# Splitting the first wq load by partitions: 16 rows of partitions ahead of the other 112

## The chip, the cores and the metric

One Trainium2 chip, one core of it. The metric is device time in microseconds for one execution of the whole kernel, as the median of several runs. Beside it there is one profiled execution, from which every duration below comes.

## What is computed

One token (x, 1 x 1024) goes through a layernorm, and the result feeds two branches whose outputs are added to x: attention over the last 4096 positions of a KV cache, and an MLP.

```python
xn = layernorm(x)
# branch A: 32 query heads, 4 KV heads, head size 128, window W = 4096
q = xn @ wq                                  # wq: 1024 x 4096
scores = q . k_cache[:, :, Sk - W:] * 128**-0.5
o = softmax(scores) . v_cache[:, :, Sk - W:]
a = o @ wo                                   # wo: 4096 x 1024
# branch B
y = layernorm(xn)
b = gelu(y @ w1 + b1) @ w2 + b2              # w1: 1024 x 3584, w2: 3584 x 1024
out = x + a + b
```

All inputs are bf16. With one token every weight is used once, so some 40 MB have to be brought in: wq, wo and the two cache windows take 8 MB (wo, wq) and 4 MB (K, V) each, w1 and w2 7 MB each.

## The kernel before

All large loads are issued by SP on one queue, in an order written out by hand; each has a semaphore that rises by 16 when it has landed. `load_rows` (L164 to 170, its DMA is L166) takes a weight matrix seen as 128 partitions x rows: for wq, partition p holds rows 8p to 8p+7 of the matrix, so "row" below means one of the 8 rows of 4096 numbers (8 KB) that a partition holds. `load_cache` (L172, L173) loads K or V.

The order on SP:

1. wq, in two chunks: one row for all partitions (1 MB), then seven rows (7 MB), into `WA` (L175).
2. After POOL has made its constants (`C["selq"]`, L210): K into `KT` (L211), w1 into `W1` (L212), V into `V` (L213).
3. After the q product (`C["q"]`, L323): w2 into `WA`, over wq (L324).
4. After the product with w1 (`C["h"]`, L424): wo in five loads, into `W1` and `KT` (L425 to 427).
5. The result (L583).

ACT issues three small loads on its own queue: x (four rows of 512 B, into partitions 0, 32, 64 and 96 of `XB4`, L191), b1 (four rows of 1,792 B into the same partitions of `B1R`, L192) and later b2 (L246).

The compute follows the loads. DVE transposes x (L242), POOL, PE, ACT and DVE make the layernorm's statistics, and `XNTb` (L261) holds the normalised x. `wide_product` (L306 to 318, its matmuls are recorded at L283) multiplies it with wq: for each chunk it waits on that chunk's semaphore and runs 8 matmuls for each row. Then q is brought into the block form `QB` (L327 to 350), DVE transposes K in four parts (L355), PE makes the scores (L363 to 371), DVE and ACT the softmax (L375 to 406), PE the product with w1 (L411 to 420), the product with V (L470 to 476), the product with w2 (L516) and at the end the product with wo chunk by chunk (L547 to 575), each waiting for its load. PE products through `go` are recorded at L292.

The lines that tie the wq chunks to the product:

```python
WQ_CHUNKS = [1, 7]
load_rows(WA, wq_p, WQ_CHUNKS, NQ, s_wq)
wide_product(WA, [(0, 1), (1, 8)], NQ, s_wq, XNTb, 512, [4, 5], "q")
```

Of the kernel before, what the change touches and what calls it, by code (L numbers as in the profile page):

```python
# [19 lines left out]
KC = D // 128  # L20
NQ = 4096
# [2 lines left out]
PB = 128  # L24
NEG = -1.0e20
PV_UNROLL = 5
WQ_CHUNKS = [1, 7]
W1_CHUNKS = [8]
W2_CHUNKS = [28]
WO_CHUNKS = [16, 8, 4, 3]  # L30
# [22 lines left out]
def bass_parallel_sum__sliding_block_cached__mixer_channel_mlp__decode_kernel(  # L53
# [18 lines left out]
    pe, dve, act, pool, sp = nc.tensor, nc.vector, nc.scalar, nc.gpsimd, nc.sync  # L72

    def sems(name, n):
        return [nc.alloc_semaphore(f"{name}{i}") for i in range(n)]

    s_x, s_b1, s_b2, s_res, s_out = (nc.alloc_semaphore(n) for n in ("s_x", "s_b1", "s_b2", "s_res", "s_out"))
    s_wq = sems("s_wq", len(WQ_CHUNKS))
    s_w1 = sems("s_w1", len(W1_CHUNKS))
# [10 lines left out]
    def sb(name, shape, d):  # L90
        return nc.alloc_sbuf_tensor(name, shape, d)

    f32, bf16 = dt.float32, dt.bfloat16
    WA = sb("WA", [128, KC * NQ], bf16)
# [21 lines left out]
    XNTb = sb("XNTb", [128, 8], bf16)  # L116
# [38 lines left out]
    wq_p = A_wq.rearrange("(p r) n -> p r n", r=KC)  # L155
# [8 lines left out]
    def load_rows(dst, src, chunks, width, semaphores, first=0, c0=0, off=0):  # L164
        for j, n in enumerate(chunks):
            sp.dma_start(  # L166
                dst[:, off + c0 * width: off + (c0 + n) * width].rearrange("p (c n) -> p c n", c=n),
                src[:, first + c0: first + c0 + n, :],
            ).then_inc(semaphores[j], 16)
            c0 += n  # L170
# [1 line left out]
    def load_cache(dst, src, sem):  # L172
        sp.dma_start(dst[:, :], src[0, :, SK - W:SK, :].rearrange("g (m b) d -> m g (b d)", m=32)).then_inc(sem, 16)  # L173

    load_rows(WA, wq_p, WQ_CHUNKS, NQ, s_wq)  # L175
    def d(ins):
        return DVE.mark(ins)

# [103 lines left out]
    def held(out, rhs, w, pos, size, start, stop, load=False):  # L282
        return pe.add_instruction(mybir.InstMatmult(  # L283
            name=nc.get_next_instruction_name(), engine=PEE, ldweights=load,
            start_tensor_calc=start, stop_tensor_calc=stop, tile_size=size, tile_position=pos,
            ins=[pe.lower_ap(rhs), pe.lower_ap(w, for_matmul_weights=True)], outs=[pe.lower_ap(out)]))
# [18 lines left out]

    def wide_product(weights, chunks, width, semaphores, vec, n, banks, name):  # L306
        for j, (k0, k1) in enumerate(chunks):
            pe.wait_ge(semaphores[j], 16)
            for k in range(k0, k1):
                w = vec[:, k:k + 1].to_broadcast([128, 32])  # L310
                for a in range(4):
                    pe.ldweights(w, tile_position=(0, 32 * a))  # L312
                for b in range(2):
                    for a in range(4):
                        lo = k * width + (2 * a + b) * n
                        last = held(PS[32 * a:32 * a + 32, banks[b] * 512: banks[b] * 512 + n], weights[:, lo:lo + n], w,
                                    (0, 32 * a), (128, 32), k == 0, k == KC - 1)
        C[name] = PE.mark(last)

    hinted = pe.mark_branch_hint_location()  # L320
    wide_product(WA, [(0, 1), (1, 8)], NQ, s_wq, XNTb, 512, [4, 5], "q")

    sp.wait_ge(PE.sem, C["q"])  # L323
    load_rows(WA, w2_p, W2_CHUNKS, D, s_w2)  # L324
# [290 lines left out]
```

## Time and profile before

| what | value |
|---|---|
| median of three runs | 98.87 us (98.68 to 98.9) |
| profiled execution, its own time | 98.68 us |
| its span in the profile | 97.4 us |
| moved by DMA | 39.88 MB, mean 410 GB/s over the span |
| busy: PE, PEld, DVE, ACT, POOL | 53.7, 14.0, 41.3, 11.5, 8.2 us |
| wq, first chunk: issue to landing | 1,024 KB, 4.5 us |
| wq, second chunk | 7,168 KB, 21.2 us |
| K, w1, V, w2: issue to landing | 25.7, 41.9, 51.1, 48.2 us |

The time is that of the device from start to end of one execution; the span is what the profile's records cover, and 1.28 us lie around it. Busy times overlap each other. The landing time of a load runs from its issue on SP, so it holds the wait behind earlier loads on the same DMA engines too. Stretches of the trace give, for any interval, the busy time of each engine, the clock granted to PE, the mean share of the 16 DMA engines that was taken, and GB/s; a DMA packet is booked in the stretch in which it starts.

### The profile page before, as it was taken

To read this page: it belongs to the slowest core of one execution; us is meant where nothing else is said; L and a number is where in the kernel's file an instruction comes from. 1 tells how busy PE (TensorE), PEld (TensorE's weight loads), DVE (VectorE), ACT (ScalarE), POOL (GpSimd) and SP (SyncE) were. 2 spreads that over 40 slices of the span, in tenths; PEclk is the share of its full clock that TensorE was granted. 3 is DMA by queue.
4 is the path that set the end of the run, shared out by engine and by line. 5 is a ranking of instruction groups with operands and counts; after the bars stand their busy time and mean duration, and the time that the engine had idled before them with its cause. 6 is when DMAs were issued, how large, how long until landed. Compare 5 with 4: busy or idle time off the path is not lost.

```text
span 97.4 us, 886 instructions
## 1 busy us (share of the span) xinstructions
PE 53.7 (55%) x361; PEld 14.0 (14%) x218; DVE 41.3 (42%) x43; ACT 11.5 (12%) x22; POOL 8.2 (8%) x33
## 2 busy tenths in 40 slices
PE   0000241007933929663366189875999577877862
PEld 0000220001200002001010022112333111212320
DVE  0001221000065899999996630599941500020021
ACT  0000517000022000000000449400000000000021
POOL 6776211000000000000000000000000000000000
PEclk9999999999996555799985555999999999999999
DMA  2998888999999988889999999888899999799980
GB/s 77 707 401 377 380 377 378 401 542 431 417 431 562 448 377 377 377 377 565 404 431 431 431 569 401 377 377 377 377 542 427 431 431 431 323 431 397 422 365 11
DMA packets 1614, 39.88 MB, mean 410 GB/s; under 512 B 190, under 2 KB 204, under 8 KB 460
## 3 DMA queue, kind: packets, MB, share of 16 engines
q1 hardware_dynamic: 1588, 39.85, 95.6%
q8 instruction: 1, 0.02, 0.1%
q10 hardware_dynamic: 24, 0.01, 0.0%
q14 instruction: 1, 0.01, 0.0%
HBM read 39.86 MB, written 0.00 MB: 409 GB/s over the span
## 4 chain that ended last, share of the span: by engine, by line
DMA 55%; DVE 22%; PE 12%; POOL 5%; issue 3%; SPq 2%; ACT 1%; POOLq 0%
DMA KT<-in_A_wo_dram 29%; DMA KT<-in_A_k_cache_dram 26%; DVE KT L355 18%; PE PS L292 8%; PE PS L283 3%; DVE MX L377 2%; SPq L166 2%; POOL F L206 1%; POOL B1R L188 1%; DVE MR L388 1%; ACT Q L381 1%; POOL QB L198 1%; DVE ORow L581 0%; PE PS L385 0%; POOL I L199 0%
## 5 line engine op out<-in xcount | busy, mean ns | idle before, releaser
L355 DVE STREAM_TRANSPOSE KT<-KT 128x4096 bf16<-128x4096 bf16 x4 | 17.4, 4413 | 1.1 <-DMA KT<-in_A_k_cache_dram 1.1
L283 PE MATMUL PS<-KT,QB 128*128 128x512 bf16 x32 | 10.4, 483 | 7.6 <-DVE KT L355 7.6
L283 PE MATMUL PS<-WA,XNTb 128*32 128x512 bf16 x64 | 6.1, 553 | 7.4 <-DMA WA<-in_A_wq_dram 7.4
L292 PE MATMUL PS<-V,WA 128*128 (+1 forms) x31 | 7.9, 381 | 1.6 <-DVE LR L430 1.4
L292 PE MATMUL PS<-WA,GT 128*32 x56 | 6.7, 382 | 2.5 <-issue 1.8
L292 PE MATMUL PS<-W,YTb 128*32 x64 | 6.7, 432 | 0.8 <-issue 0.7
L253 PE MATMUL PS<-XT,onesf 128*128 128x16 f32 x2 | 0.6, 384 | 10.6 <-POOL XT L251 10.6
L327 DVE CAST Q<-PS 128x512 bf16<-128x512 f32 x1 | 0.7, 692 | 11.9 <-PE PS L283 11.9
L242 DVE STREAM_TRANSPOSE XT<-XB 128x256 bf16<-128x256 bf16 x1 | 0.6, 626 | 9.4 <-DMA XB<-in_A_x_dram 9.4
L367 PEld LDWEIGHTS <-QB 128*128 128x128 bf16 x16 | 1.8, 114 | 18.3 <-DVE KT L355 13.8
L406 DVE STREAM_TRANSPOSE WA<-WA 128x4096 bf16<-128x4096 bf16 x1 | 4.4, 4433 | 0.0
L283 PE MATMUL PS<-MRow,ML 128*128 128x512 bf16 x8 | 3.6, 626 | 0.7 <-DVE QB L348 0.7
L557 DVE COPY KT<-PS 128x512 f32<-128x512 f32 x1 | 0.7, 692 | 7.7 <-PE PS L292 7.7
L292 PEld LDWEIGHTS PS<-V,WA 128*128 (+1 forms) x32 | 3.1, 96 | 5.9 <-issue 2.9
L292 PE MATMUL PS<-W,OT 128*32 128x512 bf16 x48 | 2.9, 380 | 1.6 <-DMA W<-in_A_wo_dram 0.9
L520 DVE TENSOR_TENSOR OD<-PS,D 128x128 f32<-128x128 f32 x1 | 0.3, 292 | 8.2 <-PE PS L518 8.2
L381 ACT ACTIVATE Q<-PS 128x512 f32<-128x512 f32 x1 | 0.6, 597 | 24.0 <-DVE MX L377 24.0
L298 PE MATMUL PS<-identf 128*128 128x512 f32 (+4 forms) x10 | 3.4, 454 | 0.0
L558 ACT ACTIVATE KT<-PS 128x512 f32<-128x512 f32 x1 | 0.6, 597 | 22.4 <-PE PS L292 22.4
L402 ACT ACTIVATE WA<-PS,NMB 128x1024 bf16<-128x1024 f32 (+1 forms) x2 | 3.1, 1535 | 1.3 <-DVE NMB L397 1.3
L312 PEld LDWEIGHTS <-XNTb 128*32 128x32 bf16 x32 | 1.1, 130 | 11.8 <-DMA WA<-in_A_wq_dram 8.3
L377 DVE TENSOR_REDUCE MX<-PS 128x1 f32<-128x2048 f32 x1 | 2.3, 2291 | 0.8 <-PE PS L283 0.8
(104 smaller groups left out, 46.3 us busy)
## 6 DMA issues: line engine op xcount, KB each, us to landing
WA<-in_A_wq_dram SPq DMA_DIRECT2D x1, 7168.0 KB, 21.2
W<-in_B_w_dram SPq DMA_DIRECT2D x1, 7168.0 KB, 41.9
WA<-in_B_w_dram SPq DMA_DIRECT2D x1, 7168.0 KB, 48.2
KT<-in_A_k_cache_dram SPq DMA_DIRECT2D x1, 4096.0 KB, 25.7
V<-in_A_v_cache_dram SPq DMA_DIRECT2D x1, 4096.0 KB, 51.1
W<-in_A_wo_dram SPq DMA_DIRECT2D x1, 4096.0 KB, 20.0
W<-in_A_wo_dram SPq DMA_DIRECT2D x1, 2048.0 KB, 24.5
WA<-in_A_wq_dram SPq DMA_DIRECT2D x1, 1024.0 KB, 4.5
```

Source lines behind the costliest of these rows:

```text
L166: sp.dma_start(dst[:, off + c0 * width: off + (c0 + n) * width].rearrange("p (c n) -> p c n", c=n), src[:, first + c0: first + c0 + n, :], ...
L188: C["b1z"] = p(pool.memset(B1R[:, :], 0.0))
L283: return pe.add_instruction(mybir.InstMatmult(name=nc.get_next_instruction_name(), engine=PEE, ldweights=load, start_tensor_calc=start, st ...
L292: return pe.add_instruction(mybir.InstMatmult(name=nc.get_next_instruction_name(), engine=PEE, ldweights=load, start_tensor_calc=start, st ...
L298: pe.matmul(bank(3, 0, n), lhsT=identf[:, :], rhs=identf[:, 0:64].unsqueeze(1).to_broadcast([128, n // 64, 64]), start=True, stop=True)
L312: pe.ldweights(w, tile_position=(0, 32 * a))
L355: C["kt"].append(d(dve.transpose(KT[:, j * W:(j + 1) * W], KT[:, j * W:(j + 1) * W])))
L367: pe.ldweights(w, tile_position=(0, 0))
L377: C["mx1"] = d(dve.tensor_reduce(out=MX[:, 1:2], in_=PS[:, 2048:4096], axis=AX.X, op=ALU.max))
L381: C["s7"] = ACT.mark(act.activation(out=S7, in_=bank(7), func=ACTF.Copy))
L402: C[f"exp{j}"] = C["exp"] = ACT.mark(act.activation(out=PT[:, lo:lo + n], in_=src, func=ACTF.Exp, bias=NMB[:, 0:1], scale=SCALE, accum_out ...
L406: C["PT"] = d(dve.transpose(PT, PT))
```

## The change

The first two wq loads become three. The first takes two rows for partitions 0 to 15 only (256 KB), the second the same two rows for partitions 16 to 127 (1.75 MB), the third the other six rows for all partitions (6 MB). The first two raise the same semaphore, and PE waits for 32 on it before the first two rows' matmuls. The chunks of the product follow: two rows, then six. Nothing else is touched.

```diff
-WQ_CHUNKS = [1, 7]
+WQ_CHUNKS = [2, 6]
+LEAD = 16
...
-    load_rows(WA, wq_p, WQ_CHUNKS, NQ, s_wq)
+    n = WQ_CHUNKS[0]
+    for lo, hi in ((0, LEAD), (LEAD, 128)):
+        sp.dma_start(WA[lo:hi, 0:n * NQ].rearrange("p (c n) -> p c n", c=n), wq_p[lo:hi, 0:n, :]).then_inc(s_wq[0], 16)
+    load_rows(WA, wq_p, WQ_CHUNKS[1:], NQ, s_wq[1:], c0=n)
...
     def wide_product(weights, chunks, width, semaphores, vec, n, banks, name):
         for j, (k0, k1) in enumerate(chunks):
-            pe.wait_ge(semaphores[j], 16)
+            pe.wait_ge(semaphores[j], 32 if j == 0 else 16)
...
-    wide_product(WA, [(0, 1), (1, 8)], NQ, s_wq, XNTb, 512, [4, 5], "q")
+    wide_product(WA, [(0, WQ_CHUNKS[0]), (WQ_CHUNKS[0], KC)], NQ, s_wq, XNTb, 512, [4, 5], "q")
```

## The prediction

> **What bounds the kernel now.** I read the slices of the span first, then the queues, the chain that ended last, the waits, and at last short stretches of the first microseconds, because the change is made there.
>
> ```profile
> DMA  2998888999999988889999999888899999799980
> ...
> q1 hardware_dynamic: 1588, 39.85, 95.6%
> ...
> DMA 55%; DVE 22%; PE 12%; POOL 5%; issue 3%; SPq 2%; ACT 1%; POOLq 0%
> ```
>
> SP's queue (q1) keeps the 16 DMA engines busy for 95.6% of the span. The chain names DVE and PE for a third of the span, but that is only the path by which the releases are followed. The stretches show the same stream without a gap:
>
> ```profile
> 6.00:30.00 24.00, 7.29 (x68) 2.06 (x36) 4.33 (x11) 4.16 (x7) 3.77 (x16) 0.99 0.98 421
> 30.00:60.00 30.00, 17.96 (x66) 3.06 (x34) 23.59 (x12) 4.25 (x7) 0.00 (x0) 0.67 1.01 434
> 60.00:94.00 34.00, 27.16 (x208) 8.40 (x124) 12.71 (x20) 2.60 (x8) 0.00 (x0) 0.99 1.00 426
> ```
>
> Each line gives the stretch, its length, the busy time of PE, PEld, DVE, ACT and POOL, PE's granted clock, and as the last two columns the DMA share and GB/s: from 6 to 94 us the engines are full at 421 to 434 GB/s, some 26.6 GB/s each. A 16 KB packet so takes 16,384 B / 26.6 = 0.62 us. The compute may not break this stream: the wo loads are issued at 65.5 us, after SP's longest wait,
>
> ```profile
> SPq L166 <- PE PS L422: 37.6, 1, 37.6
> ```
>
> and w2 lands only at 27.6 + 48.2 = 75.8, so the queue holds 10 us of work then. The end is therefore: first byte, plus 39.85 MB at the engines' rate, plus the tail from the landing at 95.37 to 97.4. Whatever moves the stream moves the end one for one; nothing else has a price unless it uses up its cover.
>
> The start, in stretches of the same view:
>
> ```profile
> 1.15:1.76 0.61, 0.00 (x0) 0.00 (x0) 0.00 (x0) 0.00 (x0) 0.61 (x1) 1.00 0.00 0
> 1.76:1.90 0.14, 0.00 (x0) 0.00 (x0) 0.00 (x0) 0.00 (x0) 0.14 (x1) 1.00 1.99 468
> 1.90:2.02 0.12, 0.00 (x0) 0.00 (x0) 0.00 (x0) 0.00 (x0) 0.06 (x2) 1.00 0.00 0
> 2.02:2.11 0.09, 0.00 (x0) 0.00 (x0) 0.00 (x0) 0.00 (x0) 0.09 (x1) 1.00 2.11 546
> ```
>
> A packet (one partition's piece of one load) is booked whole where it starts, so shares over 1 are possible. The first issue runs from 0.74 to 1.15 us; no packet starts for another 0.61 us. Then 468 GB/s x 0.14 us = 65.5 KB: eight 8 KB packets start from 1.76 to 1.90, none for 0.12 us, and 546 x 0.09 = 49 KB, six more (two records are missing), start from 2.02. So eight engines start some 0.26 us after the other eight. I read this as descriptors made one row after the other, the first half of the rows for eight engines, the second half for the others: 0.26 us for 64 rows, 4.1 ns a row. [...]
>
> **The change, part by part.** *The start.* The lead load has 16 rows. If each engine gets one, the last is made after 16 x 4.1 = 0.07 us, and the late eight engines start up to 0.26 us earlier: -0.13 us as a mean, -0.26 for the late ones. The stream does not level the engines (in the trace the 56 KB packets of one round start over 0.35 us at 4.5 us, and over 0.54 at 73), so I take -0.26, with -0.13 and -0.34 (the whole spread of starts) as ends.
>
> *The lead load's writes.* Here lies the main term. [...] The lead load puts 16 engines on partitions 0 to 15, four groups. If a group's path takes one engine's rate, four share it: 4 x 0.62 = 2.48 us for the packet instead of 0.62, and all 16 engines lose 1.86 us, which a stream at full rate cannot win back. Does a path limit exist? One event bears on it. B1R's four 1,792 B rows go to partitions 0, 32, 64 and 96. [...]
>
> ```profile
> 10.89:10.93 0.04, 0.04 (x2) 0.04 (x2) 0.00 (x0) 0.04 (x1) 0.00 (x0) 1.00 9.94 4301
> 11.07:11.08 0.01, 0.01 (x1) 0.01 (x1) 0.00 (x0) 0.01 (x1) 0.00 (x0) 1.00 13.75 5734
> 11.11:11.20 0.09, 0.09 (x1) 0.01 (x1) 0.00 (x0) 0.09 (x1) 0.00 (x0) 1.00 7.36 3186
> ```
>
> The three packets in the first stretch took 9.94 x 16 x 0.04 / 3 = 2.12 us each; the one that started at 11.07 took 13.75 x 16 x 0.01 = 2.20. One stream packet, just one, was 0.08 us longer beside some 0.14 us of foreign writing. Priced by this row (0.6 of the foreign time) the lead loses 3 x 0.62 x 0.6 = 1.1 us; with no path limit, nothing; with sixteen rows on one path, 15 x 0.62 = 9.3, for which nothing speaks. I take 1.86, since four engines stand on each path for their whole packet, and keep 0 (the first rival) and 1.1 as ends.
>
> [...]
>
> *The load of partitions 16 to 127.* 112 rows of 16 KB are seven packets for an engine, 4.3 us. If the rows stay with the engines that have them now, no path is shared and the price is 0. [...] Ends 0 and 2.2; no row tells which split holds, so I take 0.6, the middle of the first two outcomes.
>
> *One more load.* SP issues three instead of two: one issue is 0.41 us (the two wq issues took 0.87 together), and it ends at 1.97 instead of 1.56. Behind it on SP is only the k_cache load, which waits for POOL until 6.44. In the rings it adds one completion packet (9 ns): 0.02 us. ACT's issue of x starts at 1.98, just behind; even 0.5 us there is covered, next paragraph.
>
> *The wait for 32 on s_wq[0], and the chunks of 2 and 6.* PE now needs 2 MB instead of 1 MB first: about 1.76 + 5.0 to 8.0 = 7 to 10 us. PE's first q matmul is at 14.04, set by x's layernorm, so 4 us of cover remain. Nothing but q itself stands behind that wait on PE. Two rows (2.1 us) then run before the six land, near 22 to 24 us. Six rows instead of seven behind that landing: 5.10 x 6/7 = 4.4 us, so q ends 0.7 us earlier against it. That is worth nothing: w2's issue, which waits for q, joins a queue full until 58 us, and DVE already stands idle for the K cache:
>
> ```profile
> PE PS L283 <- DMA WA<-in_A_wq_dram: 7.4, 1, 7.4
> ...
> DVE KT L355 <- DMA KT<-in_A_k_cache_dram: 1.1, 1, 1.1
> ```
>
> If x came 6 us later than now, this cover would be gone and q would be late by the rest.
>
> **Sum.** -0.26 + 1.86 + 0.6 + 0.02 = +2.2 us. The profiled execution took 98.68 (span 97.4 and 1.28 around it), so 100.9; the median of the three runs is 98.87, so 101.1, which I give. With the ends of this case: 98.87 + 1.1 - 0.34 = 99.6 to 98.87 + 1.86 + 2.2 - 0.13 = 102.8.
>
> **Rivals.** *Faster: no shared path.* Every engine writes to any partition at its own rate; then only the start is left: -0.26 + 0.02, 98.6 (98.5 to 98.8 with the ends). For it: packets of 8 KB and of 56 KB alike run at the engine's rate, and B1R's rows themselves took only 74 ns, no longer than their size asks. Against it: the packet at 11.07. It decides from the point where a lead packet loses less than 0.24 us, an eighth of full sharing. 25 in 100; in a quarter of these the gain comes from the mean start, -0.11, and counts as no change.
>
> *Slower for another reason: the lead isn't spread.* If rows 0 to 15 stay with the engines that own them now, four engines get four rows each and twelve get nothing until the second load, whose issue is 0.41 us behind. No path is shared, the late eight engines start at 2.02 + 0.41 less 16 rows of descriptors: +0.34, 99.2. [...] 10 in 100.
>
> *Nothing.* Gain and loss cancel within the bound: 2 in 100.
>
> **Numbers.** A measurement of this kernel can tell some 0.2% (0.2 us) from no change. The forecast has 63 in 100. Faster: three quarters of 25, 0.19. Same: the rest of that rival and the two, 0.08. Slower: 63 + 10, 0.73. The range of 98.5 to 102.8 holds the first rival's centre, the second and the forecast's own range (99.6 to 102.8); about 12 in 100 stay outside, mostly above.
>
> **What would show it.** Right: the lead's 16 KB packets last some 2.5 us, first starts lie within 0.1 us, the 112 rows' packets are uneven, and x, K, w2 and wo all land about 2.2 us later, with the tail from the last landing still 2.0 us. Wrong: lead packets of 0.6 to 0.95 us (the first rival), or 12 engines whose first packet starts after 2.1 us (the second). It would be wrong altogether if the stream got gaps after 6 us, or if L355 were released by anything but the K cache.

## The result, and the profile after

The changed kernel takes 102.6 us (median of 6 runs, 102.45 to 102.76), the kernel before 98.78 (6 runs). The ratio is 1.0387, interval 1.0372 to 1.0402: 3.8 us slower. The profiled execution has a span of 101.2 us, before 97.4.

The page after, the same three lines (DMA slices, SP's queue, the chain by engine):

```profile
DMA  4999997977999988889959999899888999999980
...
q1 hardware_dynamic: 1604, 39.85, 95.6%
...
DMA 57%; DVE 21%; PE 11%; POOL 5%; issue 2%; SPq 2%; ACT 1%; POOLq 0%
```

The bound is the same and the queue as full as before: packets stand on the engines for 95.6% of a span that is longer. A full engine isn't a fast one: from 8 to 10 us a share of 1.03 moves 263 GB/s, from 30 to 60 us one of 1.01 moves 437, so the GB/s have to be read beside the share. Stretches of the trace after (stretch, length, busy time of five engines, clock, DMA share, GB/s):

```profile
1.75:1.85 0.10, 0.00 (x0) 0.00 (x0) 0.00 (x0) 0.00 (x0) 0.10 (x1) 1.00 5.96 1311
1.85:1.99 0.14, 0.00 (x0) 0.00 (x0) 0.00 (x0) 0.00 (x0) 0.10 (x1) 1.00 0.00 0
1.99:2.60 0.61, 0.00 (x0) 0.00 (x0) 0.00 (x0) 0.00 (x0) 0.48 (x3) 1.00 1.05 215
2.60:4.00 1.40, 0.00 (x0) 0.00 (x0) 0.00 (x0) 0.00 (x0) 1.01 (x4) 1.00 1.17 187
4.00:6.00 2.00, 0.00 (x0) 0.00 (x0) 0.00 (x0) 0.00 (x0) 1.54 (x7) 1.00 0.79 213
6.00:8.00 2.00, 0.00 (x0) 0.00 (x0) 0.00 (x0) 0.00 (x0) 1.43 (x7) 1.00 1.05 311
8.00:10.00 2.00, 0.00 (x0) 0.00 (x0) 0.00 (x0) 0.00 (x0) 1.21 (x5) 1.00 1.03 263
...
30.00:60.00 30.00, 15.15 (x59) 2.29 (x24) 25.18 (x13) 2.22 (x5) 0.00 (x0) 0.79 1.01 437
```

The loss arises here. From 2.6 to 10 us the engines move 187 to 311 GB/s instead of 410 to 430; a 16 KB packet that started between 6 and 8 us took 1.05 x 16 x 2.00 / 38 packets = 0.88 us, not 0.62. From 30 us on the rate is that of before. The start is told by the first three lines: 1311 x 0.10 = 131 KB, eight packets of 16 KB at once, then none for 0.14 us, and the other eight spread from 2.00 to 2.53. The late eight engines are not brought forward. The first 48 KB packets of the third load, which start from 10.07 to 10.91 us, still take 2.16 us in the mean, those of the next round 1.82.

After that the loss is only carried along. The K cache released DVE at 36.01 us instead of 32.09 (the chain: 6.44 + 29.57 against 6.44 + 25.65), the last wo load released PE at 99.21 instead of 95.37, and from there to the end it is 2.0 us in both. The chain's end after, with start, length and piece:

```profile
70.76 28.45 DMA KT<-in_A_wo_dram
99.21 0.04 issue
99.26 0.29 PE PS L296 x4
99.55 0.02 issue
99.58 0.42 DVE ORow L585
```

The waits after, with line numbers four higher:

```profile
PE PS L287 <- DMA WA<-in_A_wq_dram: 9.6, 1, 9.6
...
DVE KT L359 <- DMA KT<-in_A_k_cache_dram: 1.5, 1, 1.5
```

The two first rows ran at 14.87 us, set by the layernorm of x; their loads had landed by 11.8 us and were no limit. q moved with the six rows' landing, and DVE still stood idle for K after it.

### The profile page after: what moved, and what is told of

Its sections match the earlier page's. It is cut to its first block, busy times and chain, and to the rows that moved or that the text cites. A ratio compares the mean times of both kernels' runs of the same rounds, so it can differ in the third digit from the quotient of the medians.

```text
span 101.2 us, 888 instructions
## 1 busy us (share of the span) xinstructions
PE 53.6 (53%) x362; PEld 14.0 (14%) x218; DVE 41.3 (41%) x43; ACT 11.5 (11%) x22; POOL 8.2 (8%) x33
## 3 DMA queue, kind: packets, MB, share of 16 engines
q1 hardware_dynamic: 1604, 39.85, 95.6%
## 4 chain that ended last, share of the span: by engine, by line
DMA 57%; DVE 21%; PE 11%; POOL 5%; issue 2%; SPq 2%; ACT 1%; POOLq 0%
DMA KT<-in_A_k_cache_dram 29%; DMA KT<-in_A_wo_dram 28%; DVE KT L359 17%; PE PS L296 7%; PE PS L287 3%; DVE MX L381 2%; SPq L167 2%; POOL F L210 1%; POOL B1R L192 1%; DVE MR L392 1%; ACT Q L385 1%; POOL QB L202 1%; DVE ORow L585 0%; PE PS L389 0%; POOL I L203 0%
## 5 line engine op out<-in xcount | busy, mean ns | idle before, releaser
L287 PE MATMUL PS<-WA,XNTb 128*32 128x512 bf16 x64 | 6.7, 592 | 9.6 <-DMA WA<-in_A_wq_dram 9.6
L246 DVE STREAM_TRANSPOSE XT<-XB 128x256 bf16<-128x256 bf16 x1 | 0.6, 625 | 10.2 <-DMA XB<-in_A_x_dram 10.2
```

Of the source, the lines that this page charges most:

```text
L287: return pe.add_instruction(mybir.InstMatmult(name=nc.get_next_instruction_name(), engine=PEE, ldweights=load, start_tensor_calc=start, st ...
```

## Experiments

Theory, to be tested: engines that write into neighbouring partitions at the same time share a write path as fast as one DMA engine; a load of all 128 partitions leaves each engine a path of its own, other loads do not. Which partitions share a path is my assumption: no trace names the engine or the partition of a packet. Rivals: the form of the packets or the smaller chunks; a fixed price of any load with fewer than 128 partitions; a price of a third load; all of the cost in one of the two loads; and a price on the reading side, since a load of some partitions reads other addresses of wq.

**Chunks of 2 and 6 alone (e1_two_rows).**

```diff
-WQ_CHUNKS = [1, 7]
+WQ_CHUNKS = [2, 6]
...
-    wide_product(WA, [(0, 1), (1, 8)], NQ, s_wq, XNTb, 512, [4, 5], "q")
+    wide_product(WA, [(0, 2), (2, 8)], NQ, s_wq, XNTb, 512, [4, 5], "q")
```

> The chunks of 2 and 6 rows alone: one load takes two rows for all 128 partitions, no lead. Shared write paths (my theory): every engine stays on its own groups of four partitions, so the stream is as before: 98.8 us, within 0.2. Rival, the form of the packets (16 KB of two rows at a time) or the smaller chunk order is what costs: most of the 3.8 us of the change, 101 to 102.6.

Measured 98.82 us against 98.82: ratio 1.0002 (0.9992 to 1.0011). The chunks and the 16 KB packets cost nothing. What is left for the 3.8 us is the division by partitions, or the third load that comes with it (e3_columns below).

**256 KB more, to partitions 0 to 15 (d_low16), to every eighth (d_step8), to all (d_all).** Each puts one unused load ahead of the kernel before:

```diff
...
+    sp.dma_start(V[0:16, 0:2 * NQ].rearrange("p (c n) -> p c n", c=2), wq_p[0:16, 0:2, :]).then_inc(s_d, 16)
     load_rows(WA, wq_p, WQ_CHUNKS, NQ, s_wq)
...
+    sp.wait_ge(s_d, 16)
     load_cache(V, A_v_cache, s_v[0])
```

d_step8 has `V[0:128:8, 0:2 * NQ]` as destination, d_all `V[:, 0:1024]` from `wq_p[:, 0, 0:1024]`.

> The kernel before, with one load more ahead of all others: 256 KB that nobody uses, 16 KB for each of the partitions 0 to 15, into V's space (SP waits for it before V's load). The bytes alone are 262 KB / 426 GB/s = 0.62 us. Shared write paths: four engines on each of four groups, 0.62 + 1.86 = 2.5 us over before, 101.2. Rival, a load of fewer than 128 rows has a fixed price whatever its partitions: the same as d_step8. Rival, no sharing at the lead and all of the cost in the 112 rows: 0.6, 99.4.

> As d_low16, with the same 256 KB in the same 16 packets, but to partitions 0, 8, 16, ... 120. [...] Shared write paths: two engines on a path, 2 x 0.62 = 1.2 us over before, 100.0, half of d_low16. Rival, the number of rows counts: equal to d_low16. Rival, nothing is shared: 0.6, 99.4.

> As d_low16, with the same 256 KB spread over all 128 partitions, 2 KB each. Shared write paths: each engine on its own groups, so only the bytes: 0.62 to 0.7 us over before, 99.4 to 99.5. Every rival gives the same; it is the measure of the bytes for the two others.

Measured against 98.82: d_low16 100.79 (+1.97), d_step8 100.08 (+1.26), d_all 99.45 (+0.63, the bytes); each difference is known to some 0.2 us. So at this place the lead costs 1.97 - 0.63 = 1.34 us over its bytes, less than 1.86. d_step8 has the number expected, but not for the reason alone: its issue on SP took 0.63 us instead of 0.40, and its first packet started at 2.15 us instead of 1.75, 0.40 of the 0.63 over the bytes. What remains for sharing is 0.2, no more than the uncertainty. Both runs read the same bytes of wq in the same 16 packets and have fewer than 128 partitions; only the destination differs, and d_low16 costs 0.71 us more though it starts earlier. So neither the reading side nor a fixed price of short loads makes the difference between them.

**The same load behind wq (d_low16_late).** The unused load of d_low16 is issued after `load_rows(WA, wq_p, ...)` instead of ahead of it.

> The unused 256 KB for partitions 0 to 15 again, but issued behind the two wq loads, where the engines run at full rate. At the start it cost 1.97 us: 0.63 of bytes (d_all) and 1.34, not the 1.86 of full sharing. My theory: the first packets are slow in any kernel (8 KB took 0.41 to 0.69 us there, not 0.31), so a part of the sharing hides behind a start that is slow anyway; late there is no such cover: 0.62 + 1.86 = 2.5 us over before, 101.3. Rival, a path takes more than one engine's rate: 1.97 again, 100.8.

Measured 101.3 against 98.92: +2.38, over the bytes (0.63, measured at the start) 1.75, close to full sharing (1.86). The rival's 1.97 lies just under the interval, 2.02 to 2.80. Stretches of its trace: the unused load's 16 KB packets, K's 32 KB packets just behind them, and later ones:

```profile
21.60:22.20 0.60, 0.00 (x0) 0.00 (x0) 0.00 (x0) 0.00 (x0) 0.00 (x0) 1.00 2.36 437
22.40:24.30 1.90, 0.33 (x4) 0.11 (x4) 0.00 (x0) 0.00 (x0) 0.00 (x0) 1.00 1.20 276
25.20:25.36 0.16, 0.16 (x8) 0.14 (x4) 0.00 (x0) 0.00 (x0) 0.00 (x0) 1.00 1.90 819
```

437 x 0.60 is sixteen packets, 2.36 x 16 x 0.60 / 16 = 1.42 us each. The sixteen behind them took 1.20 x 16 x 1.90 / 16 = 2.28 in the mean, the four at 25.2 took 1.2. An engine's two packets so need 1.42 + 2.28 = 3.70 us, and four sharing a path would need 2.48 + 1.21 = 3.69. The sum is that of full sharing, but more than half of the price stands in the packet behind: a short load's own packets show only a part of its price. At the start less of that price shows (1.34 us against 1.75), and there packets are slow without it: in the kernel before, with no such load, the first eight 8 KB packets took 0.41 to 0.69 us and not 0.31.

**16 KB for partitions 16 to 127 as an unused load, first and behind wq (d_112, d_112_late), and its bytes over all partitions (d_112eq).** The edit is that of d_low16 with `V[16:128, 0:2 * NQ]` from `wq_p[16:128, 0:2, :]`; d_112eq puts 14 KB into each of the 128 partitions; d_112_late issues d_112's load behind wq's.

> The kernel before, with one unused load ahead of the others that has the form of the changed kernel's second load: 16 KB for each of the partitions 16 to 127, 1.84 MB. Bytes alone 1.84 MB / 426 GB/s = 4.3 us. If each engine gets seven neighbouring partitions, paths meet, and the part of the change's 3.8 us that the lead doesn't explain (3.8 - 1.34 = 2.5) shows here: 6.2 to 6.9 us over before, 105.0 to 105.7. Rival, the rows stay with their engines and the rest of the 3.8 us is due to the order of three loads: 4.3, 103.1.

> As d_112, with the same 1.84 MB as 14 KB for each of all 128 partitions. Both theories: the bytes alone, 4.3 us over before, 103.1. It is the measure for d_112.

> The unused load of d_112 (partitions 16 to 127, 16 KB each), but behind the two wq loads. At the start it cost 105.1 - 103.31 = 1.8 us over its bytes, and with the lead's 1.34 that makes 3.1 of the change's 3.8. My theory: both were measured behind the same slow start, which covers some 0.45 us only once in the changed kernel; late, the price over the bytes is 2.2 to 2.4: 105.5 to 105.8. Rival, the rest of the 3.8 comes from the engines' different lateness behind the lead, and not from the cover: 1.8 again, 105.1.

Measured: d_112 105.1 against 98.92 (+6.18), d_112eq 103.31 (+4.39), so 1.8 us over the bytes at the start, at the lower edge of the expected range and clear of the rival's nothing. d_112_late took 106.02 against 98.76 (+7.26): 2.87 over the bytes, more than the 2.2 to 2.4 I expected. The cover of the slow start explains a part. An engine has seven of these packets. At the start the first two are 0.1 us longer together than the first two of e1_two_rows, late 0.5 longer than two full-rate packets: the cover accounts for 0.4 of the 1.1 between the two runs. Another 0.5 lies in the five behind them (0.87 us each at the start, 0.97 late), and why these differ isn't shown.

**Two halves (e2_halves).** The changed kernel with

```diff
-LEAD = 16
+LEAD = 64
```

> The changed kernel with LEAD = 64: two rows for partitions 0 to 63, then for 64 to 127, then six rows for all. Shared write paths: each half lies in the groups of eight engines, but all 16 engines carry it, so two share a path throughout; 2.1 MB at half rate takes 4.9 us more, less about 0.5 that the slow start hides: 4.2 to 4.9 us over before, 103.0 to 103.7. Rival, only the odd counts (16 and 112 partitions) are slow: 98.8. Rival, one engine carries only the rows of its own groups: each half on eight engines, which then stand idle in turn only at the start: 98.8 to 99.3.

Measured 104.1 against 98.92: +5.18 (ratio 1.0518, 1.0488 to 1.0548), above the expected 4.2 to 4.9; the rivals fall. A part of the excess is no sharing: the first two issues on SP took 1.20 us instead of 0.85 in the changed kernel, and the first packet started at 2.09 us instead of 1.76, 0.33 of the 5.18. What slows the issue isn't shown. Its trace is the plainest picture of the loss. Here are e2_halves, and then e1_two_rows, from 4 to 6 us, where both load the same two rows of wq as 16 KB packets:

```profile
4.00:6.00 2.00, 0.00 (x0) 0.00 (x0) 0.00 (x0) 0.00 (x0) 1.54 (x7) 1.00 1.12 229
6.00:10.00 4.00, 0.00 (x0) 0.00 (x0) 0.00 (x0) 0.00 (x0) 2.68 (x12) 1.00 1.00 213
```

```profile
4.00:6.00 2.00, 0.00 (x0) 0.00 (x0) 0.00 (x0) 0.00 (x0) 1.54 (x7) 1.00 0.92 393
```

229 x 2.00 us is 28 packets, 1.12 x 16 x 2.00 / 28 = 1.28 us each; in e1_two_rows 48 packets of 0.61 us. The engines are at work in both, each packet takes about twice as long, and the rate is about half: sixteen engines with 16 KB in 1.28 us each move 205 GB/s. From 6 to 10 us, which is mostly the other half, the rate is 213.

**A short first load by columns (e3_columns).** Three wq loads, each for all partitions:

```diff
-    load_rows(WA, wq_p, WQ_CHUNKS, NQ, s_wq)
+    for lo, hi in ((0, NQ // 4), (NQ // 4, NQ)):
+        sp.dma_start(WA[:, lo:hi], wq_p[:, 0, lo:hi]).then_inc(s_wq[0], 16)
+    load_rows(WA, wq_p, WQ_CHUNKS[1:], NQ, s_wq[1:], c0=1)
...
-            pe.wait_ge(semaphores[j], 16)
+            pe.wait_ge(semaphores[j], 32 if j == 0 else 16)
```

> A short first load without sharing: the first row is split by columns, 2 KB for each of all 128 partitions, then the other 6 KB, both on the first semaphore; seven rows as before. It has three wq loads as the changed kernel. Shared write paths: no price for the third load beyond 0.02 us and no gain, since the first packets of the second eight engines start 0.2 us behind the first eight whatever the load: 98.8 within 0.2. Rival, a short first load brings the late engines forward by 0.26: 98.6. Rival, a third load costs by itself: over 99.0.

Measured 98.82 against 98.76: 1.0009 (0.9999 to 1.0018). A third load costs less than 0.2 us, and a short first load gains nothing. With e1_two_rows this leaves the division by partitions as the cause of the 3.8 us.

**Other places to divide (lead32, lead48).** The changed kernel with LEAD = 32 and 48. Both forecasts are my estimate by a model: each engine gets neighbouring partitions of a load, and engines that meet on a path share one engine's rate evenly, worked through packet by packet. For LEAD = 16 it gives +4.2 us for the slowest engine and +3.0 as a mean over the engines, against the measured +3.8. Which partitions lie on one path is an assumption of the model, and no run shows it.

> The changed kernel with LEAD = 32 (two rows for partitions 0 to 31, then 32 to 127, then six for all). [...] For 32 it gives +3.7 and +2.3: a little less than the change, 101.4 to 102.4. Rival, the price is that of any division by partitions, whatever the place: 102.6.

> LEAD = 48 (3 and 5 neighbouring partitions for each engine). The same model gives +6.7 for the slowest engine and +3.8 as a mean: clearly more than the change and than LEAD = 64 (which it puts at +4.2, measured +5.2): 103.5 to 105.5. Rival, the price falls steadily from 16 to 64 or is the same for all: 102.6 to 104.1.

Measured against 98.77: LEAD = 32 103.12 (+4.35), LEAD = 48 104.87 (+6.1). 48 is the worst of the four, as the model has it, and the rivals' order (all alike, or falling) is wrong. For 32 it failed: it said a little less than the change's 3.8, and it is more. The model of even sharing and neighbouring partitions names the worst place and not the best, and it isn't good to half a microsecond. A stretch of lead48, in which the engines are at their third and last packet of the first load:

```profile
4.70:5.40 0.70, 0.00 (x0) 0.00 (x0) 0.00 (x0) 0.00 (x0) 0.54 (x3) 1.00 2.21 304
```

These are thirteen 16 KB packets of 2.21 x 16 x 0.70 / 13 = 1.90 us, all nearly alike, three times 0.62. The model has between one and three engines on a path here. That all engines are slowed evenly, the model doesn't give, and no run explains it.

## Why the prediction was right, point by point

- **The number**: 102.6 us lies 0.2 us under the upper end of 102.8, with a loss of 3.8 us where 2.2 was forecast. The direction was foreseen, and that the division by partitions is what costs; the size was not. That the range held it is partly luck: it was wide enough for both rivals too, and the error of the lead (some 0.5 us too much) covered a part of what the start and the 112 partitions lacked.
- **The bound**: right. K lands 3.9 us later, the last wo load 3.8, and the end moved by as much. Two rows' wait, x (DVE's transpose at 10.2 us instead of 9.4), q and K's transposes stayed covered, as costed at nothing.
- **The lead's writes, 1.86**: the direction was right. That the 16 partitions are four groups, with a path each that four engines share, is my assumption, and no run shows it. What the runs show in its place is a price over the bytes of 1.34 us as the first load and 1.75 at full rate. The step left out that the first packets of the kernel are slow (0.41 to 0.69 us for 8 KB), which by my estimate hides a part. The ground given for it, the one longer packet at 11.07 (2.20 us, with two of b1's rows written from 11.07 and 11.10), was none: the two 56 KB packets that start from 13.02 to 13.05 us took 9.10 x 16 x 0.03 / 2 = 2.18 us, with none of b1's rows beside them. So the lower end of 1.1 has no ground in that row, and the loss is shown by the later runs alone.
- **Partitions 16 to 127, 0.6**: the term that was mis-sized. It was the middle of 0 and 1.2, and the upper end 2.2 was the better one. No run shows how 1.2 and 2.2 come about: they are my estimate for engines that write seven neighbouring partitions each and share a path evenly. The runs show 1.8 over the bytes at the start, 2.9 at full rate, some 2.3 in the changed kernel (the sum, below).
- **The start, -0.26**: wrong. I read the gap between the first eight and the second eight engines as descriptors made row by row. With 16 rows in all a gap is still there (1.82 to 2.00 us), and the second eight start no earlier than before, so the count of rows doesn't set it. Nor does it belong to the engines whatever the load, as the expectation of e3_columns has it: in e1_two_rows, with 128 rows, thirteen packets start from 1.77 to 2.03 us without a gap. e3_columns gained nothing in time either. What makes the gap isn't shown.
- **The third load, 0.02**: right within 0.2 us (e3_columns, 1.0009).
- **The sum**: 1.34 + 1.8 = 3.1 with each load alone at the start, 1.75 + 2.87 = 4.6 with each at full rate; the change's 3.8 lies between, as it would if the slow start covers a part of two loads in a row. The packets of the changed kernel divide the loss another way. Beside e1_two_rows, which loads the same two rows undivided, an engine's first two 16 KB packets take 1.05 us more in the mean (1.24 + 1.60 against 1.13 + 0.66), the other six 2.0 (0.95 against 0.61 each), and the first 48 KB packet behind them 0.3 (2.16 against 1.82). That is 3.4 us for the mean engine; the slowest sets the end. So the lead made about 1.1 of it and the other load some 2.3, as far as the packet behind a lead packet may be put down to the lead.
- **The signs**: those of the stream came, with 3.8 to 3.9 us for K, w2 and wo and a tail of 2.0 us. Those of the start did not. The lead's packets last 0.71 to 1.69 us and not 2.5, hardly more than the first ones of e1_two_rows, where the load isn't divided (1.24 and 1.13 in the mean), and the first starts lie over 0.76 us and not 0.1. Three of them, with 0.71 to 0.93 us, look like the first rival. The sign was badly chosen, since the price stands in the packet behind.
- **The rivals**: "no shared path" fell to e2_halves and d_low16_late. "The lead isn't spread" fell to the trace: sixteen 16 KB packets start within 0.8 us, and a second one on any engine only at 2.70. In d_low16, where the lead's 16 KB packets differ from wq's 8 KB, all sixteen start from 1.75 to 2.51 us, before any engine can have had two.
- **What it didn't settle**: which partitions share a path, and which engine gets which of the 112. Seven neighbours each fits the loss and the worst place at 48, not the size at 32, nor the even packet times of lead48.

## What to carry to other kernels

In a kernel bound by its stream of loads, divide a load by columns or rows of the matrix and not by partitions: here every load of a range of partitions (16, 32, 48, 64 or 112) made the stream slower while the engines looked busy, by 1.3 us over the bytes for the lead alone up to 6.1 for LEAD = 48, and loads of all 128 cost their bytes alone (e1_two_rows 1.0002, e3_columns 1.0009, d_all 0.63 us for 256 KB). Read the DMA share and the GB/s side by side, and the mean time of packets of one size; 0.61 us against 1.28 for 16 KB shows the loss in one line. Look at the packets behind a suspected load too (2.28 us instead of 1.2 in d_low16_late). And a price at the start of a kernel can be smaller than the same price in the stream (1.34 us against 1.75 for the lead), so measure it where it will stand.

## What was not expected of the hardware

- A load of 64 partitions about doubles the packet time (1.28 us in e2_halves against 0.61 in e1_two_rows), and the packet behind one of a load of 16 partitions is longer too: 2.3 us in the mean for 32 KB instead of 1.2 (d_low16_late).
- In the loads of 16 rows, the second eight packets start 0.14 us and more behind the first eight (2.00 to 2.53 us behind 1.76 to 1.82 in the changed kernel).
- A destination of every eighth partition cost SP 0.63 us to issue instead of 0.40, and its first packet came 0.4 us later. The step isn't shown to be the reason: the issues of e2_halves, without a step, took 0.57 us, and its first packet came 0.33 us later.
